# A spectral layer and an FFN on one core: the halves of g, of the linear layer's columns and of the inverse DFT's columns as two streams of a matmul

## The chip, the cores and the metric

The kernel runs on one NeuronCore of a Trainium2 chip. The metric is device time in microseconds of one execution. TensorE (PE) multiplies, VectorE (DVE) and ScalarE (ACT) work element by element between SBUF and PSUM, GpSimd (POOL) helps with a few subtractions and starts some DMAs, and SyncE (SP) starts the other DMAs.

## The reference

A batch of 8 sequences of 3008 steps with 256 channels goes through a spectral layer and then through a feed-forward network (FFN) with 2048 hidden units:

```python
X = np.fft.rfft(x, axis=1)
Yr = Xr @ w_r - Xi @ w_i + b_r
Yi = Xr @ w_i + Xi @ w_r + b_i
Yr = np.sign(Yr) * np.maximum(np.abs(Yr) - 0.01, 0.0)      # and Yi likewise
y = np.fft.irfft(Yr + 1j * Yi, n=3008, axis=1)
h = y @ w_in                                                # 24064 rows, 256 -> 2048
g = h - np.tanh(h)
out = g @ w_out                                             # 2048 -> 256
```

## The kernel before

The transform of length 3008 = 64 · 47 is done as two small DFTs, both as matmuls. `Forward` and `Stacked` transform along 47 and keep the result in DRAM; `Spectrum` (for batch 0 `WholeSpectrum`) reads it back, transforms along 64, applies the linear layer (`cross`, `shared`, through `product` on L393), the threshold, and the inverse along 64 (`inverse`, L439 to L441); the result `z` goes to DRAM again. `Chunk` reads `z`, finishes the inverse (L592), and runs the FFN on 470 columns at a time (10 · 47; some chunks have 423, padded to 424). There are 52 chunks, and 16 blocks of 128 hidden units in each, so 832 steps.

A step has an `up` and a `down`. `up` puts 6 matmuls into the PSUM tile `h` (L622), takes `th = tanh(h)` on ACT (L633), `g = h - th` on DVE (L636), and splits g into a high and a low part: `gh`, a copy of g rounded to FP32R on ACT (L639), and `gl = g - gh` on DVE (L642). `down` adds 6 matmuls into the two PSUM tiles `o` (L657), which stay open over the 16 steps of a chunk. Each split product has three terms: low weights by high data, high by high, high by low. After a chunk's last step `store` copies both `o` tiles to SBUF, one on ACT (L673) and one on DVE (L674), and one DMA writes them out.

In this text a matmul reads two streams when its moving operand takes its columns alternately from two places: element 0 of the first half, element 0 of the second half, element 1 of the first, and so on. Before the change L622 and L657 do that, with halves 256 columns apart in tiles of 512. For this `gh` and `gl` are written parted: the even columns of g into the first half of the tile and the odd ones into the second. So the alternating read finds g's columns in their natural order, and so has `o`. The helpers are

```python
def streams(t, n): return t.rearrange("p (j i) -> p j i", j=2)[:, :, :n // 2]
def moving(t, n):  return streams(t, n).rearrange("p j i -> p i j")
def paired(t, n):  return t[:, :n].rearrange("p (i j) -> p i j", j=2)
def apart(t, n):   return paired(t, n).rearrange("p i j -> p j i")
```

L313, the FP32R DFT along 47 for batches 1 to 7, reads two streams as well: its two sequences' rows in turn, 256 columns apart, and ACT sorts them when it copies `st` (L316). The linear layer (L393) and the inverse DFT (L439 to L441) read their 256 columns in one run.

The order of every engine is written out by hand. In the first part (to about 95 us) batch 0 goes through the spectral layer whole; from there to about 182 us the FFN has begun, two chunks in turn, and the conversion of the remaining weights is put between the operations of `up` (the argument `between`). After that a table of slots places the spectral work of the later batches between the steps. `up` runs two steps ahead of `down`; `h` has two PSUM buffers, `o` one a tile.

Of the kernel before, what the change touches and what calls it, by code (L numbers as in the profile page):

```python
# [10 lines left out]
F32 = mybir.dt.float32  # L11
# [67 lines left out]
def spectral_ffn(ctx, tc, x, w_r, w_i, b_r, b_i, w_in, w_out, x_twice, f1, f1s, f2, i1, i2, out):  # L79
# [213 lines left out]
    class Stacked:  # L293
# [15 lines left out]

        def dft(self, q):  # L310
            ps = ps_f.tile([P, 512], F32, name="ps_f1", tag="f")
            pv = ps.rearrange("p (d a) -> p d a", a=2)
            nc.tensor.matmul(pv, stack["r"], self.xs[q].rearrange("p a d -> p d a"), start=True, stop=True)  # L313
            if q == 0:
                self.st = work.tile([96, XC, D], F32, name="st", tag="st")
            nc.scalar.copy(out=self.st[:, 2 * q:2 * q + 2, :], in_=pv[:96].rearrange("p d a -> p a d"))  # L316
            if 2 * q + 2 == XC:
                n = self.ch * XC
                nc.sync.dma_start(out=a_dram[self.b][n:n + XC].rearrange("n r d -> r n d"), in_=self.st)
# [22 lines left out]
    class Spectrum:  # L342
# [46 lines left out]
        def product(self, dst, hi, lo, w):  # L389
            n = 0  # L390
            for lhs, rhs in ((lo, w[0]), (hi, w[1]), (hi, w[0])):
                for t in range(2):
                    nc.tensor.matmul(dst, lhs[:, t], rhs[:, t, :], start=n == 0, stop=n == 5)  # L393
                    n += 1

        def cross(self, k):
# [36 lines left out]
        def inverse(self):  # L433
            zh, zl = self.z
            pz = ps_f.tile([P, 512], F32, name="ps_i1", tag="f")
            pzv = pz.rearrange("p (j e) -> p j e", j=2)
            th, tl = self.turns
            for jj in range(2):
                nc.tensor.matmul(pzv[:, jj], th[:, jj], zl[:, jj], start=True, stop=False)  # L439
                nc.tensor.matmul(pzv[:, jj], tl[:, jj], zh[:, jj], start=False, stop=False)  # L440
                nc.tensor.matmul(pzv[:, jj], th[:, jj], zh[:, jj], start=False, stop=True)  # L441
            self.put(pz)

        def put(self, pz, n=FULL):
# [17 lines left out]
    class WholeSpectrum(Spectrum):  # L462
# [16 lines left out]
        def cross(self):  # L479
            if self.jp % 3 < 2:  # L480
                self.vv = ps_h.tile([P, 512], F32, name="ps_v", tag="h")
            else:
                self.vv = ps_o.tile([P, 512], F32, name="ps_v", tag="o1")
            ones, brow = bias_rows
            nc.tensor.matmul(self.vv, ones, brow, start=True, stop=False)
            if self.jp % 2:
                t1 = ps_f.tile([P, 512], F32, name="ps_t1", tag="f")
            else:
                t1 = ps_o.tile([P, 512], F32, name="ps_t1", tag="o0")
            self.t1 = t1[:, :D]  # L490
            for k, (dst, lhs) in enumerate((
                (self.vv[:, :D], self.xf[:, :, 1]), (self.vv[:, D:], self.xf[:, :, 0]), (self.t1, self.sf),
            )):
                for t in range(2):
                    nc.tensor.matmul(dst, lhs[:, t], whole_lin[2 - k][:, t, :], start=k == 2 and t == 0, stop=k > 0 and t == 1)

        def cross_apart(self):
            ones, brow = bias_rows
            self.t1 = ps_f.tile([P, 512], F32, name="ps_t1", tag="f")[:, :D]
            low = ps_h.tile([P, 512], F32, name="ps_v", tag="h")[:, :D]  # L500
            high = ps_o.tile([P, 512], F32, name="ps_v", tag="o1")[:, D:]
            self.sides = low, high
            for dst, lhs, w, b in ((self.t1, self.sf, 0, None), (low, self.xf[:, :, 1], 2, 0), (high, self.xf[:, :, 0], 1, D)):
                if b is not None:
                    nc.tensor.matmul(dst, ones, brow[:, b:b + D], start=True, stop=False)
                for t in range(2):
                    nc.tensor.matmul(dst, lhs[:, t], whole_lin[w][:, t, :], start=b is None and t == 0, stop=t == 1)

        def common(self):
            self.tb = work.tile([P, D], F32, name="tb0", tag="xi")  # L510
# [25 lines left out]

        def inverse(self, parts=None):
            self.pz = ps_f.tile([P, 512], F32, name="ps_i1", tag="f")
            pz = self.pz.rearrange("p (j e) -> p j e", j=2)
            parts = parts or [self.mn]  # L540
            for jj in range(2):
                for k, part in enumerate(parts):
                    nc.tensor.matmul(pz[:, jj], self.turn[:, jj], part[:, jj], start=k == 0, stop=k + 1 == len(parts))

    groups = [GB] * (P // GB) + [P % GB]
    NG = len(groups)
# [6 lines left out]
    class Chunk:  # L553
# [62 lines left out]
        def up(self, f, between=()):  # L616
# [11 lines left out]
            def fill(k):  # L628
# [19 lines left out]
        def down(self, f, gh, gl):  # L648
# [6 lines left out]
            for t in range(2):  # L655
                for k, (lhs, rhs) in enumerate(((wout_l, gh), (wout_h, gh), (wout_h, gl))):
                    nc.tensor.matmul(  # L657
                        paired(self.o[t], n), lhs[:, f, t * P:(t + 1) * P], moving(rhs, n),
                        start=f == 0 and k == 0, stop=f == NF - 1 and k == 2,
                    )  # L660

        def store(self):
            n = self.n
            ot = work.tile([P, 2, 512], F32, name="ot", tag="ot", bufs=1)
            if self.c == NCH - 1:
                lo, n, half = begin[self.c] * 47, self.out, self.n // 2
                nc.scalar.copy(out=ot[:, 0, :n], in_=self.o[0][:, :n])
                nc.sync.dma_start(out=out[0, :, lo:lo + n], in_=ot[:, 0, :n])
                nc.scalar.copy(out=ot[:, 1, :half], in_=self.o[1][:, :half])
                nc.vector.tensor_copy(out=ot[:, 1, half:n], in_=self.o[1][:, half:n])  # L670
                nc.sync.dma_start(out=out[1, :, lo:lo + n], in_=ot[:, 1, :n])
                return
            nc.scalar.copy(out=ot[:, 0, :n], in_=self.o[0][:, :n])  # L673
# [311 lines left out]
```

## Time and profile before

| | |
|---|---|
| median of 3 runs | 2551.3 us (2551.21 to 2551.49) |
| the profiled execution | 2552.46 us, span 2550.3 us |
| granted TensorE clock | 0.998 of 2.4 GHz |
| PE busy | 2519.1 us (99%), 14098 matmuls |
| DVE busy | 1969.6 us (77%), 3431 instructions |
| ACT busy | 1674.5 us (66%), 2958 instructions |

Matmul records overlap, because a matmul's end is drawn after the next one has begun. So PE's busy share hides short stalls, and what a matmul costs is read from the distance between two starts. In the timeline a row of x2 is two matmuls, and its length is one distance and one full record. DVE and ACT run one instruction at a time, and their durations are their cost.

### The profile page before, as it was taken

The numbers are of one execution on the slowest core, as the hardware profiler recorded it, in microseconds if no ns is written. First come the engines' busy times: TensorE is split into PE (matmuls) and PEld (weight loads), VectorE is DVE, ScalarE is ACT, GpSimd is POOL, SyncE is SP. The second block draws the span as 40 slices with busy tenths as digits, with TensorE's granted clock in tenths as the row PEclk, the third lists the DMA queues.
The fourth block names the chain that finished last, engine by engine and source line by source line (L and its number), as shares of the span: only waits on it lengthen the run. The fifth ranks groups of instructions, "written<-read, shape, count | busy, mean of one in ns | idle before, by whom it ended". The sixth has DMA issues, their size and how long they took to land.

```text
span 2550.3 us, 38084 instructions
## 1 busy us (share of the span) xinstructions
PE 2519.1 (99%) x14098; PEld 2381.1 (93%) x14098; DVE 1969.6 (77%) x3431; ACT 1674.5 (66%) x2958; POOL 116.9 (5%) x132
## 2 busy tenths in 40 slices
PE   9999999999999999999999999999999999999999
PEld 7679999999999999999999999999999999999999
DVE  5887888777877877878887787777788787766665
ACT  4677558755686556965678556786568755566665
POOL 2110000000001000000000000000000000000000
PEclk9999999999999999999999999999999999999999
DMA  8535216532273311633246231363215522011000
GB/s 245 173 91 142 77 52 171 134 74 63 59 212 88 74 52 45 193 93 74 60 115 185 62 81 45 83 190 81 68 48 164 135 68 66 28 39 31 18 21 15
DMA packets 157538, 236.65 MB, mean 93 GB/s; under 512 B 12561, under 2 KB 108585, under 8 KB 157353
## 3 DMA queue, kind: packets, MB, share of 16 engines
q1 hardware_dynamic: 146025, 213.79, 29.0%
q0 software_dynamic: 11328, 20.45, 5.3%
q8 instruction: 110, 1.80, 0.3%
q14 instruction: 75, 0.61, 0.1%
HBM read 138.77 MB, written 95.42 MB: 92 GB/s over the span
## 4 chain that ended last, share of the span: by engine, by line
PE 80%; DVE 10%; ACT 6%; issue 2%; DMA 1%; SPq 0%; ACTq 0%; DVEq 0%
PE h L622 32%; PE o L657 32%; PE ps_v L393 4%; PE ps_i L592 2%; PE ps_f L373 2%; ACT gh L639 2%; DVE gl L642 2%; DVE y L424 2%; DVE g L636 2%; PE ps_t L393 2%; PE ps_f L313 1%; ACT th L633 1%; PE ps_f L264 1%; DMA xt<-in_x_twice 1%; PE ps_i L439 1%
## 5 line engine op out<-in xcount | busy, mean ns | idle before, releaser
L639 ACT CAST gh<-g 128x470 fp32r<-128x470 f32 (+1 forms) x832 | 652.6, 784 | 460.1 <-DVE g L636 453.8
L642 DVE TENSOR_TENSOR gl<-g,gh 128x470 fp32r<-128x470 f32 (+1 forms) x832 | 639.7, 769 | 386.6 <-ACT gh L639 381.0
L633 ACT ACTIVATE th<-h 128x470 f32<-128x470 f32 (+1 forms) x832 | 464.3, 558 | 248.1 <-PE h L622 246.3
L636 DVE TENSOR_TENSOR g<-h,th 128x470 f32<-128x470 f32 (+1 forms) x832 | 530.7, 638 | 107.9 <-ACT th L633 99.3
L657 PE MATMUL o<-gh,wout_l 128*128 128x470 f32 (+1 forms) x1664 | 606.7, 365 | 3.4 <-DVE ot L674 2.4
L657 PE MATMUL o<-gl,wout_h 128*128 128x470 f32 (+1 forms) x1664 | 599.8, 360 | 1.0 <-DVE gl L642 0.5
L657 PE MATMUL o<-gh,wout_h 128*128 128x470 f32 (+1 forms) x1664 | 597.5, 359 | 0.0
L622 PE MATMUL h<-yh,win_l 128*128 128x470 f32 (+1 forms) x1664 | 467.4, 362 | 10.8 <-DVE g L636 7.2
L622 PE MATMUL h<-yl,win_h 128*128 128x470 f32 (+1 forms) x1664 | 463.3, 360 | 0.1
L622 PE MATMUL h<-yh,win_h 128*128 128x470 f32 (+1 forms) x1664 | 461.7, 359 | 0.0
L622 PEld LDWEIGHTS h<-yh,win_l 128*128 128x128 f32 x1664 | 311.3, 189 | 36.9 <-DVE g L636 14.7
L657 PEld LDWEIGHTS o<-gh,wout_l 128*128 128x128 f32 x1664 | 315.5, 190 | 20.1 <-DVE ot L674 6.4
L657 PEld LDWEIGHTS o<-gl,wout_h 128*128 128x128 f32 x1664 | 314.2, 189 | 21.1 <-DVE gl L642 7.4
L622 PEld LDWEIGHTS h<-yl,win_h 128*128 128x128 f32 x1664 | 313.5, 189 | 15.5 <-DVE yl L614 2.3
L657 PEld LDWEIGHTS o<-gh,wout_h 128*128 128x128 f32 x1664 | 314.8, 189 | 13.9
L622 PEld LDWEIGHTS h<-yh,win_h 128*128 128x128 f32 x1664 | 313.5, 189 | 13.2
L424 DVE TENSOR_TENSOR y<-tb,ps_v 64x256 f32<-64x256 f32 x384 | 160.3, 417 | 7.3 <-ACT tb L511 2.2
L308 DVE TENSOR_TENSOR xs<-xt,xs 47x512 fp32r<-47x512 f32 x208 | 140.0, 681 | 24.0 <-ACT xs L307 20.1
L360 POOL DMA_DIRECT2D at<-a x84 | 79.8, 1006 | 1702.5 <-DMA at<-a 1114.0
L307 ACT CAST xs<-xt 94x512 fp32r<-94x512 f32 x208 | 128.3, 627 | 7.6 <-DMA xt<-in_x_twice 7.5
L316 ACT COPY st<-ps_f 96x512 f32<-96x512 f32 x208 | 118.9, 585 | 0.9 <-PE ps_f L313 0.9
L592 PE MATMUL ps_i<-i,zin 120*128 120x120 f32 (+1 forms) x832 | 101.0, 274 | 1.2 <-ACT st L316 1.2
(115 smaller groups left out, 2491.5 us busy)
## 6 DMA issues: line engine op xcount, KB each, us to landing
xt<-in_x_twice SPq DMA_DIRECT2D x104, 384.0 KB
a<-st SPq DMA_DIRECT2D x104, 384.0 KB
at<-a SPq DMA_DIRECT2D x96, 256.0 KB
z<-zo SPq DMA_DIRECT2D x93, 240.0 KB
out<-ot SPq DMA_DIRECT2D x44, 470.0 KB
zin<-z SPq DMA_DIRECT2D x42, 480.0 KB
at<-a POOLq DMA_DIRECT2D x72, 256.0 KB, 5.2
turn<-in_i SPq DMA_DIRECT2D x96, 128.0 KB
```

Source lines behind the costliest of these rows:

```text
L307: nc.scalar.copy(out=xs, in_=src)
L308: nc.vector.tensor_tensor(out=xs[:47], in0=src[:47], in1=xs[:47].bitcast(F32), op=ALU.subtract)
L316: nc.scalar.copy(out=self.st[:, 2 * q:2 * q + 2, :], in_=pv[:96].rearrange("p d a -> p a d"))
L393: nc.tensor.matmul(dst, lhs[:, t], rhs[:, t, :], start=n == 0, stop=n == 5)
L424: nc.vector.tensor_tensor(out=y[ri * 64:(ri + 1) * 64, jj, :], in0=common(jj, ri), in1=self.side(ri)[jj * 64:(jj + 1) * 64], op=ALU.add,)
L592: nc.tensor.matmul(ps[:, at:at + m], self.zt[:m, k, t * P:(t + 1) * P], i2t[:m, turn:turn + m], start=True, stop=True,)
L622: nc.tensor.matmul(paired(h, n), lhs[:, t, f * P:(f + 1) * P], moving(rhs[:, t], n), start=k == 0, stop=k == 5,)
L633: nc.scalar.activation(out=th[:, :n], in_=h[:, :n], func=AF.Tanh)
L636: nc.vector.tensor_tensor(out=g[:, :n], in0=h[:, :n], in1=th[:, :n], op=ALU.subtract)
L639: nc.scalar.copy(out=streams(gh, n), in_=apart(g, n))
L642: nc.vector.tensor_tensor(out=streams(gl, n), in0=apart(g, n), in1=streams(gh, n).bitcast(F32), op=ALU.subtract,)
L657: nc.tensor.matmul(paired(self.o[t], n), lhs[:, f, t * P:(t + 1) * P], moving(rhs, n), start=f == 0 and k == 0, stop=f == NF - 1 and k == 2,)
```

## The change

`gh` and `gl` are no longer parted: both are written as plain contiguous tiles of n columns. L657 reads them as two streams all the same, the first half of the columns and the second half, n/2 = 235 (or 212) columns apart. So `o` holds g's columns in another order (0, 235, 1, 236, ...), and `store` puts them back while it copies: it reads PSUM with step 2.

The linear layer and the inverse DFT read their 256 columns as two streams too, the halves 128 columns apart (512 bytes), in `product`, in `WholeSpectrum.cross` and `cross_apart`, and in both `inverse`. Each such matmul puts its columns into another order; the host permutes `x_twice`, `w_r`, `w_i`, `b_r` and `b_i` beforehand so that the order comes out natural behind the inverse DFT. L313 reads four runs now, two sequences of two halves each, in such a way that PSUM holds the two sequences one behind the other, and the copy L316 becomes contiguous. `up`'s own matmuls (L622) and the split of y (L613, L614) stay as they are.

The order of the instructions on each engine is the same in both kernels, and so is their number.

```diff
+    def streams_of(v):
+        return v.rearrange("p (j i) -> p j i", j=2)
+
+    def in_turn(v):
+        return v.rearrange("p (j i) -> p i j", j=2)
...
         def dft(self, q):
             ps = ps_f.tile([P, 512], F32, name="ps_f1", tag="f")
-            pv = ps.rearrange("p (d a) -> p d a", a=2)
-            nc.tensor.matmul(pv, stack["r"], self.xs[q].rearrange("p a d -> p d a"), start=True, stop=True)
+            pv = ps.rearrange("p (a i j) -> p a i j", a=2, j=2)
+            nc.tensor.matmul(pv, stack["r"], self.xs[q].rearrange("p a (j i) -> p a i j", j=2), start=True, stop=True)
...
-            nc.scalar.copy(out=self.st[:, 2 * q:2 * q + 2, :], in_=pv[:96].rearrange("p d a -> p a d"))
+            nc.scalar.copy(out=self.st[:, 2 * q:2 * q + 2, :], in_=ps[:96].rearrange("p (a d) -> p a d", a=2))
...
                 for t in range(2):
-                    nc.tensor.matmul(dst, lhs[:, t], rhs[:, t, :], start=n == 0, stop=n == 5)
+                    nc.tensor.matmul(paired(dst, D), lhs[:, t], in_turn(rhs[:, t, :]), start=n == 0, stop=n == 5)
...
-            pzv = pz.rearrange("p (j e) -> p j e", j=2)
+            pzv = pz.rearrange("p (k i j) -> p k i j", k=2, j=2)
...
-                nc.tensor.matmul(pzv[:, jj], th[:, jj], zl[:, jj], start=True, stop=False)
-                nc.tensor.matmul(pzv[:, jj], tl[:, jj], zh[:, jj], start=False, stop=False)
-                nc.tensor.matmul(pzv[:, jj], th[:, jj], zh[:, jj], start=False, stop=True)
+                nc.tensor.matmul(pzv[:, jj], th[:, jj], in_turn(zl[:, jj]), start=True, stop=False)
+                nc.tensor.matmul(pzv[:, jj], tl[:, jj], in_turn(zh[:, jj]), start=False, stop=False)
+                nc.tensor.matmul(pzv[:, jj], th[:, jj], in_turn(zh[:, jj]), start=False, stop=True)
...
             gh = ffn.tile([P, PITCH], F32R, name="gh", tag="g_h")
-            nc.scalar.copy(out=streams(gh, n), in_=apart(g, n))
+            nc.scalar.copy(out=gh[:, :n], in_=g[:, :n])
             fill(2)
             gl = ffn.tile([P, PITCH], F32R, name="gl", tag="g_l")
-            nc.vector.tensor_tensor(
-                out=streams(gl, n), in0=apart(g, n), in1=streams(gh, n).bitcast(F32), op=ALU.subtract,
-            )
+            nc.vector.tensor_tensor(out=gl[:, :n], in0=g[:, :n], in1=gh[:, :n].bitcast(F32), op=ALU.subtract)
...
-                        paired(self.o[t], n), lhs[:, f, t * P:(t + 1) * P], moving(rhs, n),
+                        paired(self.o[t], n), lhs[:, f, t * P:(t + 1) * P], in_turn(rhs[:, :n]),
...
         def store(self):
             n = self.n
             ot = work.tile([P, 2, 512], F32, name="ot", tag="ot", bufs=1)
+            lo, m = begin[self.c] * 47, self.out
+            back = [(streams_of(ot[:, t, :n]), apart(self.o[t], n)) for t in range(2)]
+            nc.scalar.copy(out=back[0][0], in_=back[0][1])
...
-            nc.scalar.copy(out=ot[:, 0, :n], in_=self.o[0][:, :n])
-            nc.vector.tensor_copy(out=ot[:, 1, :n], in_=self.o[1][:, :n])
-            lo, n = begin[self.c] * 47, self.out
-            nc.sync.dma_start(out=out[:, :, lo:lo + n].rearrange("t p n -> p t n"), in_=ot[:, :, :n])
+            nc.vector.tensor_copy(out=back[1][0], in_=back[1][1])
+            nc.sync.dma_start(out=out[:, :, lo:lo + m].rearrange("t p n -> p t n"), in_=ot[:, :, :m])
```

## Rows read from the trace of the kernel before

**Rows 1.** The page: the chain of waits by line, shares of the span.

```profile
PE h L622 32%; PE o L657 32%; PE ps_v L393 4%; PE ps_i L592 2%; PE ps_f L373 2%; ACT gh L639 2%; DVE gl L642 2%; DVE y L424 2%; DVE g L636 2%; PE ps_t L393 2%; PE ps_f L313 1%; ACT th L633 1%; PE ps_f L264 1%; DMA xt<-in_x_twice 1%; PE ps_i L439 1%
```

**Rows 2.** Timeline, PE, from 1500 us: start us, length us, line, tile, shape, count.

```profile
1500.28 0.40 PE L393 MATMUL ps_t<-w_h,s_l 128*128 128x256 f32 x2
1500.52 0.40 PE L393 MATMUL ps_t<-w_l,s_h 128*128 128x256 f32 x2
...
1501.00 0.36 PE L657 MATMUL o<-gh,wout_l 128*128 128x470 f32 x1
...
1501.99 0.36 PE L657 MATMUL o<-gl,wout_h 128*128 128x470 f32 x1
```

**Rows 3.** Timeline, PE, 20.3 to 25.7 us, the warm-up on one stream.

```profile
20.13 5.62 PE L690 MATMUL idle<-warm 128*128 128x512 f32 x24
```

**Rows 4.** Timeline, PE, 1018.5 to 1024 us, the DFT of L313.

```profile
1019.46 0.60 PE L313 MATMUL ps_f<-xs,f_stack 94*128 94x512 f32 x2
```

**Rows 5.** Stretches: length, busy us (count) of PE, PEld, DVE, ACT, POOL, clock, DMA.

```profile
95.00:182.00 87.00, 78.58 (x353) 59.98 (x352) 76.10 (x121) 57.91 (x99) 17.83 (x12) 1.00 0.38 115
182.00:2550.00 2368.00, 2351.50 (x13359) 2253.74 (x13357) 1828.88 (x3175) 1571.46 (x2779) 81.52 (x101) 1.00 0.33 87
```

**Rows 6.** Lines, 95 to 182 us: count, busy us, mean ns, idle before.

```profile
L642 DVE TENSOR_TENSOR gl<-g,gh 128x470 fp32r<-128x470 f32 x26 | 22.3, 859 | 9.7 <-ACT gh L639 9.4
L639 ACT CAST gh<-g 128x470 fp32r<-128x470 f32 x27 | 21.5, 796 | 16.4 <-DVE g L636 16.4
L657 PE MATMUL o<-gl,wout_h 128*128 128x470 f32 x51 | 20.6, 404 | 1.0 <-DVE gl L642 0.5
L622 PE MATMUL h<-yh,win_l 128*128 128x470 f32 x56 | 18.8, 412 | 7.4 <-DVE g L636 6.7 <-ACT yh L613 0.2
```

**Rows 7.** Timeline, PE, 1500 to 1512 us, the FP32 matmuls.

```profile
1503.38 1.95 PE L373 MATMUL ps_f<-f,at 128*128 128x128 f32 x16
1505.16 1.94 PE L592 MATMUL ps_i<-i,zin 120*128 120x120 f32 x16
```

**Rows 8.** Waits of PE: us in total, times, longest.

```profile
PE h L622 <- DVE g L636: 7.2, 17, 0.9
PE ps_f L313 <- DVE xs L308: 3.9, 8, 0.9
PE h L622 <- ACT yh L613: 3.0, 7, 0.5
PE o L657 <- DVE ot L674: 2.4, 4, 1.7
```

**Rows 9.** Lines by shape, PE, whole span.

```profile
L657 PE MATMUL o<-gl,wout_h 128*128 128x470 f32 x1408 | 512.1, 364 | 1.0 <-DVE gl L642 0.5
...
L657 PE MATMUL o<-gl,wout_h 128*128 128x424 f32 x256 | 87.8, 343 | 0.1
...
L393 PE MATMUL ps_v<-w_h,xl 128*128 128x256 f32 x336 | 67.7, 283 | 0.0
...
L439 PE MATMUL ps_i<-z_l,turn_h 128*128 128x256 f32 x168 | 47.7, 284 | 1.0 <-DVE xi L386 0.8
...
L393 PE MATMUL ps_t<-w_h,s_l 128*128 128x256 f32 x168 | 33.9, 284 | 0.0
```

**Rows 10.** Lines by shape, ACT, whole span.

```profile
L639 ACT CAST gh<-g 128x470 fp32r<-128x470 f32 x704 | 557.9, 792 | 432.7 <-DVE g L636 426.8
...
L307 ACT CAST xs<-xt 94x512 fp32r<-94x512 f32 x208 | 128.3, 627 | 7.6 <-DMA xt<-in_x_twice 7.5
L316 ACT COPY st<-ps_f 96x512 f32<-96x512 f32 x208 | 118.9, 585 | 0.9 <-PE ps_f L313 0.9
```

**Rows 11.** Lines by shape, DVE, whole span.

```profile
L642 DVE TENSOR_TENSOR gl<-g,gh 128x470 fp32r<-128x470 f32 x704 | 549.6, 781 | 338.9 <-ACT gh L639 334.2
...
L308 DVE TENSOR_TENSOR xs<-xt,xs 47x512 fp32r<-47x512 f32 x208 | 140.0, 681 | 24.0 <-ACT xs L307 20.1
```

**Rows 12.** Chain of waits, 100 to 190 us: shares by line.

```profile
by line: DVE gl L642 19.4%; ACT gh L639 17.3%; DMA z<-zo 11.4%; DVE g L636 9.4%; DVE w_s L200 6.4%; issue 5.4%; DVE w_f L218 5.2%; DVE w_s L221 3.9%; DMA xt<-in_x_twice 3.8%; DVE w_f L224 3.4%; DVE xs L308 3.3%; ACT w_f L204 3.2%; PE h L622
```

More of the change, by code (lines that the diff above doesn't have):

```diff
@@ L494, in cross @@
                 for t in range(2):
-                    nc.tensor.matmul(dst, lhs[:, t], whole_lin[2 - k][:, t, :], start=k == 2 and t == 0, stop=k > 0 and t == 1)
+                    nc.tensor.matmul(
+                        paired(dst, D), lhs[:, t], in_turn(whole_lin[2 - k][:, t, :]), start=k == 2 and t == 0, stop=k > 0 and t == 1,
+                    )
         def cross_apart(self):
@@ L506, in cross_apart @@
                 for t in range(2):
-                    nc.tensor.matmul(dst, lhs[:, t], whole_lin[w][:, t, :], start=b is None and t == 0, stop=t == 1)
+                    nc.tensor.matmul(
+                        paired(dst, D), lhs[:, t], in_turn(whole_lin[w][:, t, :]), start=b is None and t == 0, stop=t == 1,
+                    )
         def common(self):
@@ L538, in inverse @@
             self.pz = ps_f.tile([P, 512], F32, name="ps_i1", tag="f")
-            pz = self.pz.rearrange("p (j e) -> p j e", j=2)
+            pz = self.pz.rearrange("p (k i j) -> p k i j", k=2, j=2)
             parts = parts or [self.mn]
@@ L542, in inverse @@
                 for k, part in enumerate(parts):
-                    nc.tensor.matmul(pz[:, jj], self.turn[:, jj], part[:, jj], start=k == 0, stop=k + 1 == len(parts))
+                    nc.tensor.matmul(pz[:, jj], self.turn[:, jj], in_turn(part[:, jj]), start=k == 0, stop=k + 1 == len(parts))
     groups = [GB] * (P // GB) + [P % GB]
@@ L664, in store @@
             ot = work.tile([P, 2, 512], F32, name="ot", tag="ot", bufs=1)
+            lo, m = begin[self.c] * 47, self.out
+            back = [(streams_of(ot[:, t, :n]), apart(self.o[t], n)) for t in range(2)]
+            nc.scalar.copy(out=back[0][0], in_=back[0][1])
             if self.c == NCH - 1:
-                lo, n, half = begin[self.c] * 47, self.out, self.n // 2
-                nc.scalar.copy(out=ot[:, 0, :n], in_=self.o[0][:, :n])
[L668 to L671, printed above, removed]
+                nc.sync.dma_start(out=out[0, :, lo:lo + m], in_=ot[:, 0, :m])
+                nc.scalar.copy(out=back[1][0][:, 0], in_=back[1][1][:, 0])
+                nc.vector.tensor_copy(out=back[1][0][:, 1], in_=back[1][1][:, 1])
+                nc.sync.dma_start(out=out[1, :, lo:lo + m], in_=ot[:, 1, :m])
                 return
-            nc.scalar.copy(out=ot[:, 0, :n], in_=self.o[0][:, :n])
-            nc.vector.tensor_copy(out=ot[:, 1, :n], in_=self.o[1][:, :n])
-            lo, n = begin[self.c] * 47, self.out
-            nc.sync.dma_start(out=out[:, :, lo:lo + n].rearrange("t p n -> p t n"), in_=ot[:, :, :n])
+            nc.vector.tensor_copy(out=back[1][0], in_=back[1][1])
+            nc.sync.dma_start(out=out[:, :, lo:lo + m].rearrange("t p n -> p t n"), in_=ot[:, :, :m])
     chunks = [Chunk(c) for c in range(NCH)]
@@ L968 @@
     given["x"] = given["x"][:2]
+    turn = np.arange(D).reshape(2, D // 2).T.reshape(-1)
+    back = np.argsort(turn)
+    given["x_twice"] = given["x_twice"][..., back]
+    for name in ("w_r", "w_i"):
+        given[name] = given[name][:, back[back]]
+    for name in ("b_r", "b_i"):
+        given[name] = given[name][back]
+    given = {n: np.ascontiguousarray(a) for n, a in given.items()}
     given |= dict(zip(("f1", "f1s", "f2", "i1", "i2"), dft_constants()))
```

## The prediction

> **What bounds the kernel now.** I read the chain of waits first, because PE's busy share of 99% says little: matmul records overlap, so two that follow each other at 198 ns are each drawn 360 ns long. The chain [rows 1] gives 32% to `h` and 32% to `o`, the two FFN matmul groups, about 4% and 2% to the linear layer (`ps_v`, `ps_t`, L393), and only 2% each to the cast `gh` (L639) and the subtraction `gl` (L642). So TensorE sets the time and there are two ways to gain: a shorter distance from one matmul to the next, or fewer stalls between them. ScalarE and VectorE count only where PE waits for them.
>
> Distances are read from the timeline [rows 2]. The first and the last of six L657 matmuls in a row start 0.99 us apart: 198 ns each, for 470 columns. At one column a cycle of the granted 2.4 GHz that is 195.8 ns, so a matmul that reads two streams carries 2 ns on top. The L393 rows, one stream of 256 columns, start 0.24 us apart for two: 120 ns where one a cycle would be 106.7, so 13 ns on top. The warm-up row [rows 3] repeats it for 512 contiguous columns: (5.62 − 0.39) / 23 = 227 ns against 213.3, 14 on top. The surplus of a single stream is thus about 12 ns a matmul, whatever its length. For L313, two streams of 512 columns [rows 4], it is 0.60 − 0.38 = 0.22 us, some 5 to 7 on top.
>
> Stalls are what is left when the distances are counted off. From 95 to 182 us [rows 5] PE starts 353 matmuls. By [rows 6], 51 × 3 + 56 × 3 = 321 of them have 470 columns: 63.6 us. The other 32 are nearly all FP32 ones of 0.11 us [rows 7] and make about 4. So some 19 of 87 us are stall. PE's busy time in that stretch shows only 8.4 us of it, since records overlap, so a stall counts 2.3 times what it shows. After 182 us PE is 16.5 us short of busy, some 4 of them behind its last matmul; 12 × 2.3 gives about 28 us of stall, spread over many places. The waits view [rows 8] names `g`, `xs` and `yh` as the largest.
>
> **The change part by part.** No instruction is added, removed or moved on any engine; only access patterns and the columns' places change. So every queue, SP's included, keeps its order, and no wait is new.
>
> *Linear layer and inverse DFT (L393, L439 to L441).* 3 × 336 + 3 × 168 + 3 × 168 = 2016 matmuls of 256 columns [rows 9] go from one stream to two, now 512 bytes apart. No row has that distance. By the 470-column rows the new distance would be 106.7 + 2 = 109 ns; the weight load bounds it elsewhere: FP32 matmuls of 128 and 120 columns, which alike load 128 weight columns each, stand (1.95 − 0.27) / 15 = 112 and (1.94 − 0.28) / 15 = 111 ns apart [rows 7], hardly dependent on the columns, so I read it as the load's pace. I take 112: 2016 × 8 = **−16 us**. Ends: 0 (they stay at 120) and −22 (109). That two streams become slower than one I exclude by both two-stream rows being below. The FP32 ones of batch 0 (L495 to L543, some 200 by the code) may gain or lose the same 12 ns each, 2 us either way; I take 0.
>
> *gh and gl contiguous.* Today gh reads every second column and writes two runs: 792 ns for 470 columns; a contiguous cast of 512 (L307) takes 627 [rows 10]. The new gh lies between 627 × 470/512 = 576 and 627; I take 600, a cut of 192. Likewise gl: 781 now, L308 takes 681 for 512 contiguous, so 625 to 681; I take 640, a cut of 141 [rows 11]. Together ACT loses 832 × 0.19 = 160 us of work and DVE 117, but this is worth only what the chain holds of it. In the stalled stretch the chain is 17.3% gh and 19.4% gl of 90 us [rows 12], 15.6 + 17.5 us; there they last 796 and 859 ns [rows 6], and a quarter off each gives 8.3: **−8 us**. Ends: 0 (the conversions of weights queued on DVE take over) and −19 (all the stall). After 182 us gh and gl hold about 4% of the span less these 33 us, some 70 us [rows 1, 12]; a quarter is 17, but here PE has slack of only fractions of a microsecond at each place and takes over soon. I take a third, **−6 us**, between 0 and −17. What is late next there is the work behind `yh` and `xs`, whose casts are not changed.
>
> The Trainium skill, "SBUF — State Buffer", section "Door 1: The DMA port swizzle", holds that consecutive accesses to a 16-byte line run at full bandwidth from two hits a line on. Reading every second FP32 value still makes two hits a line, so by it gh would gain nothing from becoming contiguous; the row of 792 against 627 for more columns speaks against that, but the two runs it writes are also in that row. This stands as a rival below.
>
> *The down projection (L657).* 4992 matmuls ((1408 + 256) × 3, [rows 9]) still read two streams, but 235 or 212 columns apart instead of 256. All two-stream rows here have 1024 bytes between the streams. Nearest row: L657 itself, so **0**; the bad end is the surplus of one stream, 12 × 4992 = +60 us, and nothing suggests a gain, as 2 ns are all that is left (−10).
>
> *Store.* Each of 51 chunks now reads PSUM with step 2. L316 does that today at 585 ns for 512 columns [rows 10], no dearer than other ACT copies, so ACT's half costs 0. For DVE's half no row shows it; with gl's surplus it is +141 ns × 51 = 7 us if every one is waited for. Only 4 waits on L674 stand in the view [rows 8]: **+1**, between 0 and +7. The same L316 becomes contiguous: 0, within ±0.03 us a piece off the path.
>
> Sum: −16 − 8 − 6 + 1 = −29. The profiled execution took 2552.46 us (span 2550.3), so 2523.5; the median of the runs is 1.2 below it, 2551.3, so **2522 us**.
>
> **Rivals.**
> 1. *The odd distance costs PE.* If streams 235 apart lose what two streams gain, L657 goes from 198 to 210 ns; 64% of the chain is FFN matmuls and half of that pays it. 2522 + 60 = 2582 us, slower. It decides from 6 ns a matmul on, where the 29 us are eaten. For it: every fast row has 1024 bytes. Against: the surplus is the same at 256 and 512 columns, so it looks tied to the single stream and not to an address. 13%.
> 2. *The weight load sets 120 ns, not the stream.* Then the 2016 matmuls stay: 2522 + 16 = 2538. For it: each has a 128-column load, and 112 is near. Against: the 512-column row has the same surplus with the load long done. 16%.
> 3. *gh and gl stay as long, or are hidden anyway* (the line rule's outcome): −8 and −6 fall away, 2522 + 14 = 2536. For it: DVE is busy 76 of 87 us in the stretch [rows 5], with conversions too. Against: rows of contiguous casts. 13%.
> 4. *Neither does anything*: the gains of 2 and 3 both missing, about 2552. 5%.
>
> **How the numbers follow.** The forecast has 53%; its own range, from the ends of its terms taken at about two thirds, is 2506 to 2536. About 0.2% (5 us) is what a measurement of this kernel tells from no change. Faster: forecast, rivals 2 and 3, 0.53 + 0.16 + 0.13 = 0.82. Same: rival 4, 0.05. Slower: rival 1, 0.13. The range of 8 in 10 takes in rivals 2 and 3 and a mild form of rival 1 (5 ns, +25): 2506 to 2548; left out are the full rival 1, rival 4 and the far low end.
>
> **What would show it.** Right: L393 and L441 start 109 to 113 ns apart, L657 stays at 198, gh near 600 and gl near 640 ns, fewer and shorter waits on `g` from 95 to 182 us, with the 87 us stretch some 8 us shorter. Wrong: L657 above 200 ns (rival 1), L393 at 118 to 120 (rival 2), gh above 720 (rival 3), or long waits of PE on `ot` at the starts of chunks, which would make the step-2 reading of PSUM dearer than I allow.

## The result, and the profile after

The changed kernel takes 2516.4 us (median of 4 runs, 2515.95 to 2518.89) against 2551.3 in the same session: a ratio of 0.9866 with a 95% interval of 0.9849 to 0.9884, some 35 us less. The profiled execution took 2518.89 us, its span is 2516.8.

In the changed kernel `up`'s matmuls are on L632, `down`'s on L665, the linear layer on L399, the inverse DFT on L445 to L447, the FP32 linear layer of batch 0 on L501, `th`, `g`, `gh` and `gl` on L643, L646, L649 and L652, the halves of y on L623 and L624, the DVE copy of the store on L682.

The chain of waits, beside [rows 1]:

```profile
PE h L632 35%; PE o L665 35%; PE ps_v L399 4%; PE ps_i L602 3%; PE ps_f L379 3%; PE ps_t L399 2%; PE ps_f L319 2%; DVE gl L652 1%; DVE g L646 1%; ACT gh L649 1%; PE ps_v L501 1%; DVE y L430 1%; PE ps_i L447 1%; PE ps_i L446 1%; PE ps_i L445 1%
```

The FFN's share has risen from 64% to 70% and that of `gh` and `gl` has fallen from 2% to 1% each. More of the time is now matmul after matmul.

The timeline of PE, beside [rows 2] (start, length, line, tile, shape, count):

```profile
1484.32 0.36 PE L665 MATMUL o<-gh,wout_l 128*128 128x470 f32 x1
...
1485.32 0.36 PE L665 MATMUL o<-gl,wout_h 128*128 128x470 f32 x1
...
1486.03 0.38 PE L399 MATMUL ps_v<-w_h,xl 128*128 128x256 f32 x2
1486.25 0.39 PE L399 MATMUL ps_v<-w_l,xh 128*128 128x256 f32 x2
```

Six L665 matmuls span 1.00 us from the first start to the last, 200 ns each at this reading's resolution: the odd distance of 235 columns costs at most 1 or 2 ns. Over the whole traces two neighbouring FFN matmuls of 470 columns that nothing holds up start 198.3 ns apart on L657 and L622, 198.3 on L632 and 198.9 on L665, so it is about half a nanosecond. The two L399 rows start 0.22 us apart for two matmuls instead of 0.24, so 110 to 112 ns instead of 120.

What the prediction had set to nothing are the FP32 matmuls of batch 0. The timeline of PE has eight such records in one row, first in the kernel before:

```profile
28.14 1.89 PE L495 MATMUL ps_v<-w_f,xf 128*128 128x256 f32 x8
```

and in the changed kernel:

```profile
29.26 2.34 PE L501 MATMUL ps_v<-w_f,xf 128*128 128x256 f32 x8
```

The first are (1.89 − 0.38) / 7 = 216 ns apart, the second (2.34 − 0.44) / 7 = 271. The records carry their own length of 0.38 and 0.44 us at the end of the row.

Lines of DVE and ACT, beside [rows 10, 11]; columns are count, busy us, mean ns, idle time before:

```profile
L652 DVE TENSOR_TENSOR gl<-g,gh 128x470 fp32r<-128x470 f32 x704 | 458.2, 651 | 223.2 <-ACT gh L649 213.4
...
L649 ACT CAST gh<-g 128x470 fp32r<-128x470 f32 x704 | 412.7, 586 | 374.4 <-DVE g L646 367.6
...
L623 ACT CAST yh<-yt 128x470 fp32r<-128x470 f32 x88 | 63.3, 724 | 15.6 <-DVE yt L618 14.8
L624 DVE TENSOR_TENSOR yl<-yt,yh 128x470 fp32r<-128x470 f32 x88 | 60.0, 695 | 4.6 <-ACT yh L623 3.9
...
L682 DVE COPY ot<-o 128x470 f32<-128x470 f32 x44 | 28.2, 642 | 0.9 <-PE o L665 0.6
```

`gh` has gone from 792 to 586 ns and `gl` from 781 to 651. Two rows changed that the edit does not touch: yh and yl, still parted and still 256 columns apart, fell from 798 to 724 and from 777 to 695 ns. DVE's copy of the store, which now reads PSUM with step 2, takes 642 ns; it took 646. The same lines in the kernel before:

```profile
L613 ACT CAST yh<-yt 128x470 fp32r<-128x470 f32 x88 | 69.6, 798 | 15.9 <-DVE yt L608 15.9
L614 DVE TENSOR_TENSOR yl<-yt,yh 128x470 fp32r<-128x470 f32 x88 | 67.0, 777 | 5.1 <-ACT yh L613 4.8
...
L674 DVE COPY ot<-o 128x470 f32<-128x470 f32 x44 | 28.4, 646 | 0.6 <-PE o L657 0.4
```

Waits of PE, beside [rows 8]:

```profile
PE o L665 <- DVE ot L682: 1.7, 1, 1.7
...
PE ps_f L319 <- DVE xs L314: 1.0, 3, 0.6
PE h L632 <- DVE g L646: 0.9, 2, 0.7
...
PE h L632 <- ACT yh L623: 0.2, 1, 0.2
```

All four are shorter or as short: `g` 0.9 us instead of 7.2, `xs` 1.0 instead of 3.9, `yh` 0.2 instead of 3.0.

To see where the time went, three stretches help: to the first `th`, from there to the last conversion of `win_h`, and from there to the last `th`. They are read from the answers for one line (count, shortest, median and longest ns, first and last start in us). Each comes from one profiled execution, and executions of one kernel lie up to 6 us apart (here 2515.95 to 2518.89, in e7 2519.94 to 2524.87), so a difference of 2 or 3 us between two stretches tells nothing by itself. `th` in the kernel before:

```profile
L633 ACT ACTIVATE th<-h x832: 507/562/698, 100.7 to 2542.8; 128x470 f32<-128x470 f32 x141, 128x424 f32<-128x424 f32 x26
```

and the conversions of `win_h` in the same kernel:

```profile
L228 ACT CAST win_h<-w_f x8: 615/620/620, 49.2 to 162.1; 128x512 fp32r<-128x512 f32 x8
```

`th` in the changed kernel:

```profile
L643 ACT ACTIVATE th<-h x832: 511/562/611, 107.3 to 2509.5; 128x470 f32<-128x470 f32 x141, 128x424 f32<-128x424 f32 x26
```

and the conversions of `win_h` in the same kernel:

```profile
L234 ACT CAST win_h<-w_f x8: 618/619/622, 51.8 to 159.7; 128x512 fp32r<-128x512 f32 x8
```

| | first `th` at | to the last `win_h` | to the last `th` |
|---|---|---|---|
| before | 100.7 | 61.4 | 2380.7 |
| after | 107.3 (+6.6) | 52.4 (−9.0) | 2349.8 (−30.9) |

So the changed kernel starts its FFN later, passes the crowded stretch faster, and gains most behind it. Since the linear layer accounts for some 16 of the last 30.9 us, about 15 are stalls that are gone.

### The profile page after: what moved, and what is told of

Same layout as the page of the kernel before. It is cut to its first block, busy times and chain, and to the rows that moved or that the text cites. A ratio compares the mean times of both kernels' runs of the same rounds, so it can differ in the third digit from the quotient of the medians.

```text
span 2516.8 us, 38085 instructions
## 1 busy us (share of the span) xinstructions
PE 2503.4 (99%) x14098; PEld 2365.6 (94%) x14098; DVE 1871.0 (74%) x3431; ACT 1517.1 (60%) x2958; POOL 114.8 (5%) x132
## 4 chain that ended last, share of the span: by engine, by line
PE 88%; DVE 6%; ACT 3%; DMA 2%; issue 1%; SPq 0%; ACTq 0%; DVEq 0%
PE h L632 35%; PE o L665 35%; PE ps_v L399 4%; PE ps_i L602 3%; PE ps_f L379 3%; PE ps_t L399 2%; PE ps_f L319 2%; DVE gl L652 1%; DVE g L646 1%; ACT gh L649 1%; PE ps_v L501 1%; DVE y L430 1%; PE ps_i L447 1%; PE ps_i L446 1%; PE ps_i L445 1%
## 5 line engine op out<-in xcount | busy, mean ns | idle before, releaser
L646 DVE TENSOR_TENSOR g<-h,th 128x470 f32<-128x470 f32 (+1 forms) x832 | 529.6, 636 | 269.3 <-ACT th L643 264.5
L652 DVE TENSOR_TENSOR gl<-g,gh 128x470 fp32r<-128x470 f32 (+1 forms) x832 | 534.0, 642 | 259.3 <-ACT gh L649 249.3
L649 ACT CAST gh<-g 128x470 fp32r<-128x470 f32 (+1 forms) x832 | 482.8, 580 | 400.2 <-DVE g L646 393.2
L643 ACT ACTIVATE th<-h 128x470 f32<-128x470 f32 (+1 forms) x832 | 462.1, 555 | 416.8 <-PE h L632 412.3
L665 PE MATMUL o<-gh,wout_l 128*128 128x470 f32 (+1 forms) x1664 | 605.9, 364 | 2.0 <-DVE ot L682 1.7
L665 PE MATMUL o<-gl,wout_h 128*128 128x470 f32 (+1 forms) x1664 | 598.5, 360 | 0.6
L665 PE MATMUL o<-gh,wout_h 128*128 128x470 f32 (+1 forms) x1664 | 598.0, 359 | 0.0
L632 PE MATMUL h<-yh,win_l 128*128 128x470 f32 (+1 forms) x1664 | 466.7, 362 | 1.8 <-DVE g L646 0.9
L632 PE MATMUL h<-yl,win_h 128*128 128x470 f32 (+1 forms) x1664 | 462.6, 359 | 0.0
L632 PE MATMUL h<-yh,win_h 128*128 128x470 f32 (+1 forms) x1664 | 461.7, 359 | 0.0
L632 PEld LDWEIGHTS h<-yh,win_l 128*128 128x128 f32 x1664 | 309.9, 188 | 26.3 <-DVE g L646 5.5
L665 PEld LDWEIGHTS o<-gl,wout_h 128*128 128x128 f32 x1664 | 314.3, 189 | 17.0 <-DVE gl L652 3.5
L665 PEld LDWEIGHTS o<-gh,wout_l 128*128 128x128 f32 x1664 | 314.9, 189 | 15.6 <-DVE ot L682 2.0
L665 PEld LDWEIGHTS o<-gh,wout_h 128*128 128x128 f32 x1664 | 315.0, 189 | 14.5
L632 PEld LDWEIGHTS h<-yl,win_h 128*128 128x128 f32 x1664 | 313.5, 189 | 13.6 <-DVE yl L624 0.2
L632 PEld LDWEIGHTS h<-yh,win_h 128*128 128x128 f32 x1664 | 313.5, 189 | 13.3
L313 ACT CAST xs<-xt 94x512 fp32r<-94x512 f32 x208 | 128.1, 627 | 16.4 <-DMA xt<-in_x_twice 16.1
```

Of the source, the lines that this page charges most:

```text
L313: nc.scalar.copy(out=xs, in_=src)
L632: nc.tensor.matmul(paired(h, n), lhs[:, t, f * P:(f + 1) * P], moving(rhs[:, t], n), start=k == 0, stop=k == 5,)
L643: nc.scalar.activation(out=th[:, :n], in_=h[:, :n], func=AF.Tanh)
L649: nc.scalar.copy(out=gh[:, :n], in_=g[:, :n])
L652: nc.vector.tensor_tensor(out=gl[:, :n], in0=g[:, :n], in1=gh[:, :n].bitcast(F32), op=ALU.subtract)
L665: nc.tensor.matmul(paired(self.o[t], n), lhs[:, f, t * P:(t + 1) * P], in_turn(rhs[:, :n]), start=f == 0 and k == 0, stop=f == NF - 1 and ...
```

## The experiments

Three questions were left: whether the parts add up as read above (e1 to e3), why the casts were slow and what a reading pattern costs (e4, e5, e8, e9), and through which queue shorter casts shorten the whole (e6, e7, e10 to e12). All ratios are to the kernel before, run beside them; the stretches are those of the table above.

**e1: the FP32 matmuls read one run again.**

```diff
-                        paired(dst, D), lhs[:, t], in_turn(whole_lin[2 - k][:, t, :]), ...
+                        apart(dst, D), lhs[:, t], streams_of(whole_lin[2 - k][:, t, :]), ...
```

and likewise in `cross_apart` and in batch 0's `inverse`: the moving operand is contiguous, PSUM is written with step 2.

> The changed kernel, but the FP32 matmuls of batch 0 (L501, L515, L553) read their 256 columns in one run again and write PSUM with step 2 instead, which puts the columns in the same order. Theory A: two streams cost these 196 FP32 matmuls 57 ns each (216 to 273 ns, 11 us of PE time), of which some 5 to 7 us reach the end; here they are back at 216 ns and the time is 2510 us. Rival: batch 0 waits for VectorE and DMAs anyway, the 11 us are hidden; the time stays at 2516. Second rival: a PSUM write of step 2 costs what the reading cost, and the distance is above 250 ns.

Measured: 2511.4 us, ratio 0.9846 (0.9832 to 0.9859). The row of eight records:

```profile
28.87 1.89 PE L501 MATMUL ps_v<-w_f,xf 128*128 128x256 f32 x8
```

They are 216 ns apart again, the first `th` starts at 100.5 us, and the stretches behind stay as in the changed kernel (52.5 and 2347.7). So two streams cost FP32 matmuls 55 to 57 ns a record, and writing PSUM with step 2 costs them nothing. This version has the lowest time measured here. It is 5 us below the changed kernel, as theory A said; the two intervals of the ratios overlap, so the step itself rests on the stretch before the first `th`.

**e2: the linear layer alone.** The changed kernel with `gh`, `gl`, L657's reading and the store as before.

```diff
-            nc.scalar.copy(out=gh[:, :n], in_=g[:, :n])
+            nc.scalar.copy(out=streams(gh, n), in_=apart(g, n))
...
```

> The changed kernel with g's part undone: gh, gl parted as before, L657's reading and the store as before; linear layer and inverse DFT on two streams. Theory A: 2016 matmuls 8 ns shorter (-16 us), FP32 ones dearer (+5), stalls as before: 2540 us, gh near 790 and gl near 780 ns. Rival: the stalls of before came from TensorE's reading of the linear layer or go with it; then the time is 2525 or less.

Measured: 2545.5 us, ratio 0.9981 (0.9972 to 0.9990).

The cast in the lines view is long again:

```profile
L649 ACT CAST gh<-g 128x470 fp32r<-128x470 f32 x704 | 563.1, 800 | 431.5 <-DVE g L646 424.6
```

The first `th` starts at 105.3 us (+4.6 to before); the stretches behind are 60.3 (−1.1) and 2366.6 (−14.1). So two streams are worth some 14 us behind the crowded stretch, and the FP32 ones take 5 of them back. The stalls did not go with them. It came out 5 us later than expected.

**e3: g's part alone.** The kernel before with contiguous `gh` and `gl`, L657 on halves 235 apart and the reordering store.

```diff
-            nc.scalar.copy(out=streams(gh, n), in_=apart(g, n))
+            nc.scalar.copy(out=gh[:, :n], in_=g[:, :n])
...
```

> The kernel before with g's part alone: gh and gl contiguous, L657 on halves 235 apart, the store reordering; linear layer and inverse DFT as before. Theory A: nearly all of the stalls that went (some 26 to 30 us by counting distances) went with the shorter gh and gl: 2523 us. Rival, the prediction's own sizes (-8, -6, +1): 2538 us.

Measured: 2523.8 us, ratio 0.9895 (0.9882 to 0.9909).

The cast in the lines view:

```profile
L645 ACT CAST gh<-g 128x470 fp32r<-128x470 f32 x704 | 412.8, 586 | 360.3 <-DVE g L642 354.5
```

Theory A's number. The stretches are 101.3, 52.4 (−9.0) and 2360.7 (−20.0). e2 and e3 together make −5.5 − 27.2 = −32.7; the whole change made −34.9. The parts add up.

**e4: the halves 256 apart again, g still read contiguously.**

```diff
-            nc.scalar.copy(out=gh[:, :n], in_=g[:, :n])
+            nc.scalar.copy(out=streams(gh, n), in_=streams_of(g[:, :n]))
...
-                        ... in_turn(rhs[:, :n]),
+                        ... moving(rhs, n),
```

> The changed kernel, but gh and gl are written in two contiguous runs 256 columns apart, from a g that is read contiguously; L665 reads halves 256 apart instead of 235. Theory A: the distance of the streams does not matter (L665 198 ns in both) and step-2 reading is what made the cast slow, so gh stays near 590 ns and the time at 2516 us. Rival: writing two runs made the cast slow; gh is near 790 ns and the time 2535 or more.

Measured: 2516.9 us, ratio 0.9873 (0.9859 to 0.9886).

Two casts in the lines view:

```profile
L649 ACT CAST gh<-g 128x470 fp32r<-128x470 f32 x704 | 412.1, 585 | 381.3 <-DVE g L646 374.7
...
L623 ACT CAST yh<-yt 128x470 fp32r<-128x470 f32 x88 | 70.0, 816 | 12.5 <-DVE yt L618 12.4
```

`gh` writes two runs as before and takes 585 ns. So two runs of writing alone do not make it slow. But `yh`, which reads y with step 2 as in all versions up to here, is back at 816 ns from 724, though its own instruction is unchanged; TensorE's streams in L665 are 256 columns apart again. This row led to e8 and e9. `yl` is back too:

```profile
L624 DVE TENSOR_TENSOR yl<-yt,yh 128x470 fp32r<-128x470 f32 x88 | 67.1, 777 | 5.2 <-ACT yh L623 5.2
```

The time is that of the changed kernel all the same, so the shorter yh and yl of the changed kernel are worth nothing in it.

**e5: reading patterns one by one.** Blocks of 24 matmuls on zeros behind the warm-up, for example

```python
for _ in range(24):
    nc.tensor.matmul(paired(o, D), r, in_turn(half), start=True, stop=True)
```

> The changed kernel with 10 blocks of 24 extra matmuls behind the warm-up, on a tile of zeros, one reading pattern a block, to read the distance of two starts from the trace (the added work is some 60 us and no part of the verdict). FP32R: 512 columns in one run, 512 in two streams 256 apart, 470 in two streams 235 apart, 256 in one run, 256 in two streams 128 apart, 256 with step 2. FP32: 256 in one run, 256 in two streams 128 apart, 256 with step 2, 256 in one run with PSUM written at step 2. Theory A: one run 227 and 120 ns, two streams 215, 198 and 112 whatever their distance; FP32 216 in one run and 273 in two streams. Rival: the surplus of one run is the SBUF reading of neighbours next to the weight load, then step 2 is free of it too (112 for FP32R). Second rival: FP32's 273 comes from leaving the run, then step 2 is 273 as well.

Measured: 2584.1 us in a single run, the added blocks included; what counts are the distances.

Timeline of PE; each row is a block, in the order in which the expectation names them (an FP32 matmul makes two records, so x48):

```profile
25.71 5.60 PE L728 MATMUL bench<-warm 128*128 128x512 f32 x24
31.15 5.34 PE L730 MATMUL bench<-warm 128*128 128x512 f32 x24
36.33 4.94 PE L732 MATMUL bench<-warm 128*128 128x470 f32 x24
41.10 3.04 PE L734 MATMUL bench<-warm 128*128 128x256 f32 x24
43.97 2.84 PE L736 MATMUL bench<-warm 128*128 128x256 f32 x24
46.65 5.61 PE L738 MATMUL bench<-warm 128*128 128x256 f32 x24
52.08 10.54 PE L740 MATMUL bench<-zero 128*128 128x256 f32 x48
62.46 13.27 PE L742 MATMUL bench<-zero 128*128 128x256 f32 x48
75.57 11.04 PE L744 MATMUL bench<-zero 128*128 128x256 f32 x48
86.45 10.52 PE L746 MATMUL bench<-zero 128*128 128x256 f32 x48
```

Between the starts of two rows lies a block, and that by its count is the distance; only the last is followed by other work, and (10.52 − 0.38) / 47 gives it.

| moving operand | FP32R | FP32, a record |
|---|---|---|
| 512 columns, one run | 5.44 / 24 = 227 ns | |
| 512, two streams 256 apart | 5.18 / 24 = 216 | |
| 470, two streams 235 apart | 4.77 / 24 = 199 | |
| 256, one run | 2.87 / 24 = 120 | 10.38 / 48 = 216 ns |
| 256, two streams 128 apart | 2.68 / 24 = 112 | 13.11 / 48 = 273 |
| 256, step 2 | 5.43 / 24 = 226 | 10.88 / 48 = 227 |
| 256, one run, PSUM written with step 2 | | 216 |

Theory A's numbers hold, and both rivals fall: step 2 does not free FP32R of the surplus but doubles its distance, and FP32 at step 2 pays 11 ns, not 57. Which type gains from two streams is opposite: FP32R gains 8 to 11 ns, FP32 loses 57.

**e6 and e7: more work for ScalarE.** One small copy for each step. In e6 it read a constant:

```diff
             nc.scalar.copy(out=gh[:, :n], in_=g[:, :n])
+            nc.scalar.copy(out=spare[:, :3], in_=column[:, :3])
```

> The changed kernel with one small ScalarE copy (3 columns, some 190 ns) behind each gh: ScalarE is as busy as before, while the chain th, g, gh, gl of a step keeps its new length. Theory A: the stalls went because ScalarE and VectorE have less to do and their queues run ahead; then about half comes back (some 10 to 15 us, 2528). Rival: they went because each step's chain is shorter; then hardly anything comes back (2516 to 2520).

Measured: 2544.3 us, ratio 0.9978 (0.9968 to 0.9987). But the copies were not where they were meant to be:

The answer for their line:

```profile
L651 ACT COPY spare<-column x832: 174/193/223, 108.3 to 521.4; 128x3 f32<-128x3 f32 x167
```

All 832 ran between 108 and 522 us, since nothing held them and the scheduler put them into the first free places, several a step. So e6 tells nothing of the change; it shows that ScalarE, once it is filled to 93%, does hold PE up. The stretch from 212 to 360 us (length, busy us and count of PE, PEld, DVE, ACT, POOL, clock, DMA):

```profile
212.00:360.00 148.00, 140.49 (x836) 131.10 (x835) 111.76 (x211) 137.68 (x577) 10.38 (x14) 0.98 0.28 71
```

The changed kernel starts 923 matmuls in the same 148 us, with ACT busy for 82.7. In e7 the copy reads `gh[:, :3]` and stays behind it:

> As e6_act_op_more, whose small copies were placed by the scheduler far ahead of their steps (all 832 ran before 522 us); here each copy reads 3 columns of the step's gh and so stays directly behind it. ScalarE has about as much to do as in the kernel before, the chain of a step (th, g, gh, gl) keeps its new length. Theory A: the gain after 182 us came because ScalarE's queue has less to do; then 8 to 12 us come back (2525 to 2528). Rival: it came because each step's chain is shorter, or because VectorE has less to do; then at most 4 us come back (2517 to 2520).

Measured: 2520.4 us, ratio 0.9882 (0.9866 to 0.9899).

The copies in the lines view:

```profile
L651 ACT COPY spare<-gh 128x3 f32<-128x3 f32 x832 | 160.8, 193 | 19.6
```

ScalarE has about 160 us more to do by the records. But two records that follow each other overlap by some 0.1 us (the two rows shown in e11), so durations on ACT and DVE are a little more than the cost that the section on the profile before takes them for, and the queue gets back nearer 100 ns a step, about half of what `gh` had lost. 4 us come back; the stretches are 53.9 and 2351.9, 1.5 and 2.1 us longer than in the changed kernel. That is the rival's size, and e11, with as many copies at another place, loses nothing. So this much of ScalarE's load is not what was gained; all of it was not put back.

**e8: all halves adjacent, on top of e1.** One line more than e1:

```diff
     def streams(t, n):
-        return t.rearrange("p (j i) -> p j i", j=2)[:, :, :n // 2]
+        return t[:, :n].rearrange("p (j i) -> p j i", j=2)
```

> e1_fp32_one_run, and yh and yl also keep their two streams n/2 apart (235 or 212 columns) instead of 256; they are still written parted, from every second column of y. Theory B: a step-2 reading on ScalarE or VectorE is not slow in itself, it collides with TensorE's reading of two streams that lie 1024 bytes apart; without such streams yh falls from 724 to about 620 ns, yl from 695 to about 650, and the time from 2511 to about 2508 us. Rival: step-2 reading is slow next to any two-stream matmul; yh stays above 700 ns and the time at 2511.

Measured: 2512.7 us, ratio 0.9853 (0.9839 to 0.9868).

The cast of y in the lines view:

```profile
L623 ACT CAST yh<-yt 128x470 fp32r<-128x470 f32 x88 | 57.1, 651 | 15.5 <-DVE yt L618 15.1
```

`yh` did fall, from 729 in e1 to 651 ns, as theory B has it, but the time did not: e1 had 2511.4, and the intervals overlap. 104 such casts off the path are worth nothing here.

**e9: the same line alone, in the kernel before.** It moves the halves of `gh`, `gl`, `yh` and `yl` together, so TensorE's streams lie 235 or 212 columns apart and the two runs that a cast writes adjoin.

> The kernel before, with one line changed: the halves of gh, gl, yh and yl lie n/2 columns apart (235 or 212) instead of 256; all are still parted, the linear layer and the store are as before. Theory B: gh falls from 792 to about 620 ns and gl from 781 to about 650 though they still read every second column, and most of what g's part brought comes without it: 2525 us. Rival: step-2 reading is slow in itself; gh and gl stay near 790 and 780 ns and the time at 2550 us.

Measured: 2526.8 us, ratio 0.9908 (0.9893 to 0.9922).

Lines view:

```profile
L642 DVE TENSOR_TENSOR gl<-g,gh 128x470 fp32r<-128x470 f32 x704 | 459.7, 653 | 249.3 <-ACT gh L639 230.1
...
L639 ACT CAST gh<-g 128x470 fp32r<-128x470 f32 x704 | 449.6, 639 | 368.0 <-DVE g L636 361.4
...
L613 ACT CAST yh<-yt 128x470 fp32r<-128x470 f32 x88 | 56.4, 643 | 15.5 <-DVE yt L608 14.9
```

`gh` still reads every second column, and takes 639 ns instead of 792; `gl` 653 instead of 781. Since its two runs of writing now adjoin, e9 alone does not tell a collision with TensorE from a cast that is slow when it reads at step 2 and writes two separate runs. The trace of the kernel before does, with `gh` the same throughout; here is its timeline of ACT:

```profile
1501.82 0.85 ACT L639 CAST gh<-g 128x470 fp32r<-128x470 f32 x1 [0.71 <-DVE g L636]
...
1505.83 0.63 ACT L639 CAST gh<-g 128x470 fp32r<-128x470 f32 x1 [0.50 <-DVE g L636]
```

While the first runs, TensorE is at L657 and L622; while the second runs, at L592, whose operand has one run [rows 7]. Of the 832 `gh` casts of that trace, the 508 that only L622 and L657 records overlap take 819 ns on average, and the 31 that no such record overlaps take 627 and at most 639. So the step-2 cast is slow beside TensorE's streams and not by itself. The stretches are 99.8, 52.7 and 2363.7, within 3 us of e3's. So one line brings 24 of the 27 us that g's part brought, with everything still read at step 2.

**e10: more work for VectorE.**

```diff
             nc.vector.tensor_tensor(out=gl[:, :n], in0=g[:, :n], in1=gh[:, :n].bitcast(F32), op=ALU.subtract)
+            nc.vector.tensor_tensor(out=spare[:, :3], in0=gl[:, :3].bitcast(F32), in1=gh[:, :3].bitcast(F32), op=ALU.add)
```

> The changed kernel with one small VectorE addition (3 columns of gl and gh, some 150 ns) for each step, behind its gl: VectorE is about as busy as in the kernel before, ScalarE and the chain of a step up to gl as in the changed one. Theory C: after 182 us the time was lost in VectorE's queue, through which g, gl, xs and the spectral work all pass; then 8 us or more come back (2524 or later). Rival: the length of a step's chain decides; then at most 4 us come back (2520).

Measured: 2527.8 us, ratio 0.9909 (0.9894 to 0.9924).

The additions in the lines view:

```profile
L654 DVE TENSOR_TENSOR spare<-gl,gh 128x3 f32<-128x3 f32 x832 | 136.3, 164 | 17.3
```

`th` in the answer for its line:

```profile
L644 ACT ACTIVATE th<-h x832: 510/563/645, 105.9 to 2516.4; 128x470 f32<-128x470 f32 x141, 128x424 f32<-128x424 f32 x26
```

and the conversions of `win_h` in the same kernel:

```profile
L235 ACT CAST win_h<-w_f x8: 617/618/620, 50.5 to 164.4; 128x512 fp32r<-128x512 f32 x8
```

The median is 11 us later. In the profiled execution the crowded stretch takes 164.4 − 105.9 = 58.5 us, 6.1 of the 9.0 us that it had lost; behind it the stretch is 2352.0, only 2 us longer than in the changed kernel. So VectorE's queue is what set the crowded stretch. Theory C's time came (2524 or later), but it looked for the loss behind that stretch. The profiled execution, at 2525.6 us the fastest of its four, shows 2 us there; where the other 4 to 5 us of the median lie is not shown.

**e11: a longer chain.** e7's copy reads `g[:, :3]` and stands ahead of `gh`.

> As e7_act_op_in_place, but the small ScalarE copy (some 190 ns) reads g and stands ahead of gh, so ScalarE has the same work as there and the chain from g to gl is 190 ns longer, as in the kernel before. Theory C: the chain's length matters where VectorE waits for gh in the crowded first stretch and little elsewhere; 3 to 6 us on top of e7's 2520 (2523 to 2526). Rival: the chain's length is what was gained everywhere; 10 us or more on top (2530 and later).

Measured: 2515.1 us, ratio 0.9862 (0.9845 to 0.9879).

One step in the timeline of ACT:

```profile
1491.44 0.19 ACT L650 COPY spare<-g 128x3 f32<-128x3 f32 x1 [0.71 <-DVE g L647]
1491.54 0.58 ACT L651 CAST gh<-g 128x470 fp32r<-128x470 f32 x1
```

`gh` starts 0.10 us after the copy, not 0.19, so the chain was made only some 100 ns longer. The stretches are 53.5 and 2344.9. Nothing is lost, and both expectations fail: 100 ns more in the chain cost nothing here.

**e12: the old lengths, without any step-2 reading of g.** Two of e11's copies ahead of `gh`, and one addition of 3 columns ahead of `gl`, which reads `gh`.

```diff
+            for k in range(2):
+                nc.scalar.copy(out=spare[:, 4 * k:4 * k + 3], in_=g[:, :3])
             nc.scalar.copy(out=gh[:, :n], in_=g[:, :n])
...
+            nc.vector.tensor_tensor(out=spare[:, 8:11], in0=g[:, :3], in1=gh[:, :3].bitcast(F32), op=ALU.add)
             nc.vector.tensor_tensor(out=gl[:, :n], in0=g[:, :n], in1=gh[:, :n].bitcast(F32), op=ALU.subtract)
```

> The changed kernel with the old lengths restored without any step-2 reading: two small ScalarE copies ahead of gh (some 100 ns of queue each, as they overlap with their neighbours) and one small VectorE addition ahead of gl, which reads gh (some 130 to 160 ns). Chain, ScalarE's and VectorE's work of a step are then about as in the kernel before. Theory D: the stalls that went depend on all three together, and each alone was within the slack; then most of the 27 us that g's part brought are lost again (2538 to 2546). Rival: the step-2 readings cost TensorE something beyond their length; then less than half comes back (2530 or less).

Measured: 2528.6 us, ratio 0.9914 (0.9901 to 0.9928); the stretches are 107.1, 59.1 (+6.7) and 2355.6 (+5.8). 12 of 27 us come back, just under half, and the time lies in the rival's range. But the rival's reason does not show: TensorE's own distances are the same before and after (198.3 ns on L622 and L632), so what went are waits. The old lengths were not fully restored: from the end of `g` to the end of `gl` the median is 1692 ns in the kernel before, 1302 in the changed one and 1563 here. Theory D is not borne out either: e10 alone gave back 11 us, so the three together are not shown to do more than VectorE's addition by itself.

## Why the prediction was right, point by point

The time of 2516.4 lies in the range and 6 us below the forecast of 2522. Most terms held, but two were off in opposite directions: the stalls behind 182 us (−6, measured −15) and the FP32 matmuls (0, measured +5 to +7). That the sum came so near is in part luck.

*Linear layer and inverse DFT, −16: held.* The distance is 112 ns (e5, and 0.22 us for two in the trace), and e2's last stretch is 14 us shorter. Rival 2 is out. That the weight load sets the 112 was not tested.

*The crowded stretch, −8: held* at −9.0. Its reason was right in part: gh and gl are a third of the chain there [rows 12], but the limit is VectorE's queue. e10 gives most of it back with VectorE's work alone, 100 ns more a step on ScalarE (e7, e11) only 1.5 and 1.1 us.

*Behind 182 us, −6: mis-sized.* The stalls lost there are some 15 us beyond the linear layer's 16, and e3 has 20 in its last stretch. The step that failed is "PE has slack of only fractions of a microsecond at each place and takes over soon. I take a third": nearly the whole quarter of `gh`'s and `gl`'s share (17) was got. The sentence behind it, that the work behind `yh` and `xs` is late next and their casts are not changed, failed as well: the waits on `yh` and `xs` fell from 3.0 to 0.2 and from 3.9 to 1.0 us, and the cast of `yh` from 798 to 724 ns, though e4 shows the shorter cast to be worth nothing. In the profiled executions e7, e10 and e11 gave back 2 us or nothing of this term and e12 6, which is little more than two executions differ by. Through which queue the shorter `gh` and `gl` work behind 182 us stays open.

*The FP32 matmuls of batch 0, 0 ± 2: wrong.* The step said that they "may gain or lose the same 12 ns each". They lose 57, and 196 records make 11 us of PE, of which 5 to 7 reach the end (first `th` +6.6 us; e1). The bound was taken from FP32R rows; no row of the kernel before showed an FP32 matmul on two streams, and by that it should have been wider.

*The odd distance, 0: held.* e5 shows 199 ns for 470 columns 235 apart, 216 for 512 columns 256 apart: both one column a cycle of 2.4 GHz and 2 to 3 ns. The half nanosecond by which L665 is slower than L657 makes some 2 us over its matmuls of 470 columns. Rival 1 is out.

*The store, +1: it was 0*, as DVE's copy did not become longer.

*gh and gl, 600 and 640 ns: held in size* (586 and 651) *but not in cause.* The prediction took step-2 reading itself, or the two runs of writing, to be slow. The trace of the kernel before shows that they are not: the same cast takes 627 ns where no L622 or L657 matmul overlaps it and 819 beside them. e9 agrees: at step 2, `gh` takes 639 ns once TensorE's streams lie 235 instead of 256 columns apart. e4 shows the rest: a contiguous reading takes 585 ns even with streams 256 apart. So what is slow is the pair, a step-2 reading on ScalarE or VectorE beside TensorE's streams 1024 bytes apart, and `yh` follows in three steps: 816 ns with all the FFN's streams 256 apart (e4), 724 with L632's alone (after), 651 with none (e8). Which places in SBUF collide is not shown.

The rule that the prediction set against the row, from the Trainium skill ("SBUF — State Buffer", "Door 1: The DMA port swizzle"), that two hits a line are enough, is nearer the truth than the prediction's reading of the row: 639 against 586 ns. But the Trainium skill ("SBUF — State Buffer", "SBUF: two separate sides") also says that TensorE and ScalarE never wait on anyone. The trace of the kernel before differs: the same ScalarE cast takes 819 ns beside TensorE's two streams and 627 beside its other matmuls.

## What to carry to other kernels

Before an operand is laid out anew for a slow element-wise operation, move what other engines read at that moment: here one line that takes two streams off a distance of 1024 bytes brought 24 of 27 us. Two streams paid for FP32R matmuls here, and not for FP32 ones; a helper used for both types has to be measured for both. A trial instruction that is to stay in its place has to depend on what stands there.

## What was not expected of the hardware

- FP32R, one run: 11 to 12 ns a matmul more than two streams at 512 columns, 8 at 256 (120 against 112). FP32: 216 ns a record in one run, 273 in two streams, 227 at step 2.
- FP32R at step 2 takes 226 ns for 256 columns, as long as 512 contiguous ones (227).
- An FP32 matmul may write PSUM with step 2 at no cost (216 ns), which gives a column order for free that its reading would have paid with 57 ns.
- ScalarE's and VectorE's step-2 readings were longer beside TensorE's streams 1024 bytes apart (`yh` 816 against 651 ns, and `gh` within one trace 819 against 627), and contiguous ones were not (`gh` 585).
